# A decode kernel on one core: V pieces ahead of the output projection, turns by group of four, x added late

## The chip, the cores and the metric

One core of a Trainium2 chip. The metric is device time in microseconds (us). A run's time is about 1.7 us longer than the span of its profiled execution, which the views below are cut from; the runs are all of the same (fast) state as far as a single core can tell. Where fractions of a microsecond matter I compare spans and times of day in the profile ("at 1335.4" means 1335.4 us after the span's start).

Words used below. A **piece** is a 4 MB load (K, V or a weight) into one of five slots that are used in turn. A **turn** is the small fp32 matmul step that brings the attention output of a piece from rows to columns (`oT`). **Rows** are the 16 small matmuls (`o_rows`) that then lay it out for the output projection, whose weight is `wo`. V60 to V63 are the last V pieces; wo is 8 MB. `flush()` runs the turns that are pending. PE is TensorE (PEld its weight loads), DVE VectorE, ACT ScalarE, POOL GpSimd; PSUM is the memory that matmuls add up in. The **granted clock** is the share of TensorE's full clock that the trace records.

## The reference

Four decode positions attend to 32 heads and 8192 cached positions each; a gated feed-forward part and x itself are mixed in:

```python
q = (x @ wq)                                     # 4 x 4096, heads of 128
p = softmax(q . k_cache / sqrt(128))             # K and V caches: 4 x 32 x 8192 x 128 bf16, 268 MB each
a = (p . v_cache) @ wo                           # wo: 4096 x 1024
b = x + sigmoid(x . w_r) * ((silu(x @ w_gate) * (x @ w_up)) @ w_down)
out = g * a + (1 - g) * b                        # g = sigmoid(x . gate_w)
```

## The kernel before

The parts that matter. `acc` is one PSUM sum of 4 x 1024 that takes x, the feed-forward part and the output projection.

```python
    def gates():
        # [...] g, 1-g and the sigmoid of x.w_r; then x joins the sum first:
        xf = ttp.tile([Bn, D], F32, name="xf", tag="T")
        nc.vector.tensor_copy(out=xf[:], in_=x6[0:Bn])
        dg = const.tile([Bn, Bn], F32)
        nc.vector.tensor_tensor(out=dg[:], in0=ident[0:Bn, 0:Bn], in1=c12[0:Bn, 0, :], op=ALU.mult)
        for n in range(NH):
            mm_acc(acc[:, n * NB:(n + 1) * NB], dg[:], xf[:, n * NB:(n + 1) * NB], start=True)

    def wo_piece(g0, g1, r0=0, r1=FR):          # one DMA, and a function that uses it
        w = slot()[...]
        nc.sync.dma_start(out=w..., in_=wov[:, g0:g1, r0:r1]...)
        def use():                              # 8 matmuls of 128x512 for each g (1 MB of wo)
            ...
        return use

    def v_piece(u):                             # u = 4 * g + t
        # [...] load; the last V piece in four parts
        o_ps = ops.tile([NM, 4 * Dh], F32, name="o_ps")
        # [...] 32 matmuls into o_ps; flush() after the first 8
        o_sb = osp.tile([NM, 4 * Dh], F32, name="o_sb")
        nc.scalar.copy(out=o_sb[:], in_=o_ps[:])
        def finish():                           # the turn of this piece: 8 rows to 2 columns
            for q in range(4):
                nc.tensor.matmul(oT[:, HT * t:HT * t + HT], lhsT=o_sb[:, q * Dh:(q + 1) * Dh],
                                 rhs=ident[0:NM, q:NM:4], start=(q == 0), stop=(q == 3))
            # [...] after the fourth piece of a group: scale into OT
        pending.append(finish)

    for u in range(NT + LAG):                   # NT = 64, LAG = 4
        if u < NT:
            k_piece(u)
        if u == NT + 1:
            flush()
            o_rows(0, GE)
            wo_piece(0, GS)()                   # 4 MB of wo between V60 and V61
        if u >= LAG:
            v_piece(u - LAG)
        # [...] feed-forward pieces in the first turns
    early = wo_piece(GS, GE)                    # 2 MB
    late = [wo_piece(GE, NWB - 1), wo_piece(NWB - 1, NWB, 0, FR - 1), wo_piece(NWB - 1, NWB, FR - 1, FR)]
    flush()
    early()
    o_rows(GE, NWB)
    for use in late:
        use()
```

Of the kernel before, what the change touches and what calls it, by code (L numbers as in the profile page):

```python
# [9 lines left out]
BF = mybir.dt.bfloat16  # L10
F32 = mybir.dt.float32
U32 = mybir.dt.uint32
ACT = mybir.ActivationFunctionType
ALU = mybir.AluOpType
# [5 lines left out]
def kernel(  # L20
# [22 lines left out]
    nc = tc.nc  # L43
    P = 128
    Bn, Sq, D = A_x.shape
    _, H, Sk, Dh = A_k_cache.shape
    F = B_w_gate.shape[1]
    DT = D // P
    HT = 2
    JR = Sk * HT // P  # L50
    JC = JR // 16
    GT = 4
    GH = GT * HT
# [3 lines left out]
    NT = Bn * H // HT  # L57
    LAG = 4
    FR = 4
    FG = F // (P * FR)  # L60
    NB = 512
# [5 lines left out]
    x2 = A_x.rearrange("b s d -> (b s) d")  # L67
    out2 = out.rearrange("b s d -> (b s) d")

    const = ctx.enter_context(tc.tile_pool(name="const", bufs=1))  # L70
    ring = ctx.enter_context(tc.tile_pool(name="ring", bufs=5))
    ttp = ctx.enter_context(tc.tile_pool(name="ttp", bufs=2))
    ptp = ctx.enter_context(tc.tile_pool(name="ptp", bufs=2))
    osp = ctx.enter_context(tc.tile_pool(name="osp", bufs=2))
    stat = ctx.enter_context(tc.tile_pool(name="stat", bufs=3))
    shrp = ctx.enter_context(tc.tile_pool(name="shrp", bufs=1, space=PSUM))
    accp = ctx.enter_context(tc.tile_pool(name="accp", bufs=1, space=PSUM))
# [1 line left out]
    ops = ctx.enter_context(tc.tile_pool(name="ops", bufs=2, space=PSUM))  # L79
    o2p = ctx.enter_context(tc.tile_pool(name="o2p", bufs=1, space=PSUM))  # L80

    def slot():
        return ring.tile([P, RING], BF, name="piece", tag="piece")
# [3 lines left out]
    x6 = const.tile([NX, D], BF)  # L87
# [7 lines left out]
    ident = const.tile([P, P], F32)  # L95
# [11 lines left out]
    for he in range(4):  # L107
        half, e = divmod(he, 2)
        nc.gpsimd.affine_select(out=R[:, he, :], in_=R[:, he, :], compare_op=ALU.not_equal, fill=1.0,  # L109
                                base=-(64 * half + e), pattern=[[0, 4], [-2, 32]], channel_multiplier=1)  # L110
# [3 lines left out]
                            base=0, pattern=[[-JC, GT], [-32, NQ]], channel_multiplier=1)  # L114
    nc.gpsimd.affine_select(out=m32[:], in_=m32[:], compare_op=ALU.is_ge, fill=0.0,
                            base=JC - 1, pattern=[[JC, GT], [32, NQ]], channel_multiplier=-1)
# [3 lines left out]
    nc.vector.tensor_scalar(out=pen8[:], in0=mask8[:], scalar1=-1.0, scalar2=3.0e38, op0=ALU.add, op1=ALU.mult)  # L120
    nmask8 = const.tile([P, GH], F32)
    nc.vector.tensor_scalar(out=nmask8[:], in0=mask8[:], scalar1=-scale, scalar2=None, op0=ALU.mult)
    ZW = 31 + P + 1
    Zt = [const.tile([P, 4, ZW], BF, name=f"Z{i}") for i in range(2)]
    PB = [const.tile([P, 32, 4, HT, 4], BF, name=f"PB{i}") for i in range(2)]
    for z in Zt + PB:
        nc.gpsimd.memset(z[:], 0.0)  # L127

    qT = const.tile([P, H, Bn], BF)
# [1 line left out]
    OT = const.tile([P, H, Bn], BF)  # L131
    LT = const.tile([P, FR, H // FR, Bn], BF)
    hT = const.tile([P, FG, FR, Bn], BF)
    sgb = const.tile([P, 2, Bn], F32)
# [8 lines left out]
    acc = accp.tile([Bn, D], F32)  # L143

    def mm_acc(out_ap, lhsT, rhs, start=False):
        nc.tensor.matmul(out_ap, lhsT=lhsT, rhs=rhs, start=start, stop=True, skip_group_check=True)  # L146


    def gates():
        wrep = ttp.tile([P, 2, DT, P], BF, name="wrep", tag="T")  # L150
        for i in range(2):
            nc.vector.tensor_copy(out=wrep[:, i, :, :], in_=xw[:, :, Bn + i:Bn + i + 1].to_broadcast([P, DT, P]))
            for t in range(DT):
                mm_acc(rg_ps[:, i, :], wrep[:, i, t, :], xT[t])
        nc.scalar.activation(out=sgb[:], in_=rg_ps, func=ACT.Sigmoid)
        nc.vector.tensor_scalar(out=c12[:, 0, :], in0=sgb[:, 1, :], scalar1=-1.0, scalar2=1.0, op0=ALU.mult, op1=ALU.add)
        nc.vector.tensor_tensor(out=c12[:, 1, :], in0=c12[:, 0, :], in1=sgb[:, 0, :], op=ALU.mult)
        xf = ttp.tile([Bn, D], F32, name="xf", tag="T")
        nc.vector.tensor_copy(out=xf[:], in_=x6[0:Bn])  # L159
        dg = const.tile([Bn, Bn], F32)  # L160
        nc.vector.tensor_tensor(out=dg[:], in0=ident[0:Bn, 0:Bn], in1=c12[0:Bn, 0, :], op=ALU.mult)
        for n in range(NH):
            mm_acc(acc[:, n * NB:(n + 1) * NB], dg[:], xf[:, n * NB:(n + 1) * NB], start=True)


    wqv = A_wq.rearrange("(c t) n -> c t n", t=DT)
# [37 lines left out]
    def wd_piece(g0, ng):  # L204
        w = slot()[:, :ng * FR * D].rearrange("p (g r n) -> p g r n", g=ng, r=FR)
        nc.sync.dma_start(out=w.rearrange("p g r n -> p g (r n)"),
                          in_=wdv[:, g0:g0 + ng].rearrange("f g r n -> f g (r n)"))
        for g in range(ng):
            for r in range(FR):
                for n in range(NH):  # L210
                    mm_acc(acc[:, n * NB:(n + 1) * NB], hT[:, g0 + g, r, :], w[:, g, r, n * NB:(n + 1) * NB])

    WB = P * FR // Dh
    NWB = H // WB

    def o_rows(g0, g1):

        n = g1 - g0
        lp = ops.tile([P, FR, n, Bn], F32, name="o_ps")
        for k in range(WB):  # L220
            for r in range(FR):
                nc.tensor.matmul(lp[32 * k:32 * k + 32, r], lhsT=identb[:, r:P:FR],
                                 rhs=OT[:, WB * g0 + k:WB * g1:WB, :], start=True, stop=True, skip_group_check=True)
        nc.vector.tensor_copy(out=LT[:, :, g0:g1, :], in_=lp[:])

    def wo_piece(g0, g1, r0=0, r1=FR):
        ng, nr = g1 - g0, r1 - r0
        w = slot()[:, :ng * nr * D].rearrange("p (g r n) -> p g r n", g=ng, r=nr)
        nc.sync.dma_start(out=w.rearrange("p g r n -> p g (r n)"),
                          in_=wov[:, g0:g1, r0:r1].rearrange("p g r n -> p g (r n)"))  # L230

        def use():
            for g in range(ng):
                for r in range(nr):
                    for n in range(NH):
                        mm_acc(acc[:, n * NB:(n + 1) * NB], LT[:, r0 + r, g0 + g, :], w[:, g, r, n * NB:(n + 1) * NB])
        return use
# [1 line left out]

    S_ps = {}  # L240
    rinv_t = {}
    oT_t = {}
    pending = []

    def flush():
        while pending:
            pending.pop(0)()

    def heads(u):
        return divmod(u * HT, H)  # L250

    def kv_view(cache, u):
        b, h0 = heads(u)
        return cache[b, h0:h0 + HT].rearrange("h (r j) d -> (h r) (j d)", j=JR)
# [61 lines left out]
    NM = 4 * HT  # L316

    def v_piece(u):
        b, h0 = heads(u)
        g, t = divmod(u, GT)  # L320
        B_ = PB[g % 2]
        vn = slot()
        vv = kv_view(A_v_cache, u)
        cut = 4 if u == NT - 1 else 1
        for c in range(cut):
            lo, hi = c * RING // cut, (c + 1) * RING // cut
            nc.sync.dma_start(out=vn[:, lo:hi], in_=vv[:, lo:hi])
        o_ps = ops.tile([NM, 4 * Dh], F32, name="o_ps")
        n = 0
        for jc in range(JC):  # L330
            for uq in range(4):
                j0 = 16 * jc + 4 * uq
                nc.tensor.matmul(o_ps[:, :], lhsT=B_[:, JC * t + jc, uq].rearrange("p s j -> p (s j)"),  # L333
                                 rhs=vn[:, j0 * Dh:(j0 + 4) * Dh], start=(n == 0), stop=(n == JR // 4 - 1))
                n += 1
                if n == 8:
                    flush()
        o_sb = osp.tile([NM, 4 * Dh], F32, name="o_sb")
        nc.scalar.copy(out=o_sb[:], in_=o_ps[:])  # L339

        def finish():
            if t == 0:
                oT_t[g] = o2p.tile([P, GH], F32, name="oT")
            oT = oT_t[g]
            for q in range(4):
                nc.tensor.matmul(oT[:, HT * t:HT * t + HT], lhsT=o_sb[:, q * Dh:(q + 1) * Dh],  # L346
                                 rhs=ident[0:NM, q:NM:4], start=(q == 0), stop=(q == 3))
            if t == GT - 1:
                oT_t.pop(g)
                hg = h0 + HT - GH  # L350
                nc.vector.scalar_tensor_tensor(out=OT[:, hg:hg + GH, b], in0=oT[:, :], scalar=sgb[:, 1, b:b + 1],  # L351
                                               in1=rinv_t.pop(g)[:], op0=ALU.mult, op1=ALU.mult)
        pending.append(finish)


    gates()
    wq_piece(0)
    wq_piece(TW)
# [1 line left out]
    side = [lambda: gu_piece(wgv, 0, 0), lambda: gu_piece(wgv, 0, TW), lambda: gu_piece(wuv, 1, 0),  # L360
            lambda: (gu_piece(wuv, 1, TW), h_done()), lambda: wd_piece(0, 4), lambda: wd_piece(4, FG - 4)]
    GE = NWB - GH // WB
    GS = GE // 2 + 1
    for u in range(NT + LAG):
        if u < NT:
            k_piece(u)
        if u == NT + 1:
            flush()
            o_rows(0, GE)
            wo_piece(0, GS)()  # L370
        if u >= LAG:
            v_piece(u - LAG)
        if side:
            side.pop(0)()
    early = wo_piece(GS, GE)
    late = [wo_piece(GE, NWB - 1), wo_piece(NWB - 1, NWB, 0, FR - 1), wo_piece(NWB - 1, NWB, FR - 1, FR)]
    flush()
    early()
    o_rows(GE, NWB)
    for use in late:  # L380
        use()
    res = const.tile([Bn, D], BF)
    nc.vector.tensor_copy(out=res[:, 0:NB], in_=acc[:, 0:NB])
# [33 lines left out]
```

## Time and profile before

| | before |
|---|---|
| median of the first 3 runs | 1357.39 us (1356.31 to 1358.82) |
| span of the profiled execution | 1354.7 us |
| PE busy | 1119.6 us, 83% |
| read from HBM | 575.7 MB |

DMA is full in every slice but the last, at about 431 GB/s. The kernel is bound by its load stream, and only the start and the tail can give anything.

The tail in the timeline of PE before (start us, length us, line, operation, count, and in brackets idle time and what ended it):

```profile
1307.48 7.07 PE L146 MATMUL acc<-piece,LT 128*4 128x512 bf16 x32 [0.99 <-DMA piece<-in_A_wo_dram]
1317.20 8.50 PE L333 MATMUL o_ps<-piece,PB_139 128*8 128x512 bf16 x32 [2.65 <-DMA piece<-in_A_v_cache_dram]
1326.42 1.05 PE L346 MATMUL oT<-ident,o_sb 8*128 8x2 f32 x8 [0.72 <-ACT o_sb L339]
1327.40 8.80 PE L333 MATMUL o_ps<-piece,PB_139 128*8 128x512 bf16 x40
...
1337.10 5.34 PE L333 MATMUL o_ps<-piece,PB_139 128*8 128x512 bf16 x24
1343.16 1.05 PE L346 MATMUL oT<-ident,o_sb 8*128 8x2 f32 x8 [0.72 <-ACT o_sb L339]
...
1344.88 6.85 PE L146 MATMUL acc<-piece,LT 128*4 128x512 bf16 x31
```

The first 4 MB of wo are used at 1307.5, V61 at 1317.2, V62 and V63 from 1327.4 to 1342.4, then turn and rows, then the other 32 projection matmuls to 1351.7; result and store take 3 us more.

The last microseconds of the stream, by windows (columns: window, length, busy us and count of PE, PEld, DVE, ACT, POOL, granted clock, DMA share, GB/s):

```profile
1315.00:1320.00 5.00, 2.80 (x7) 0.87 (x7) 0.00 (x0) 0.00 (x0) 0.00 (x0) 0.67 0.98 421
1344.00:1345.00 1.00, 0.67 (x20) 0.56 (x21) 0.29 (x2) 0.00 (x0) 0.00 (x0) 1.00 0.34 133
1345.00:1346.00 1.00, 1.00 (x7) 0.38 (x5) 0.14 (x1) 0.00 (x0) 0.00 (x0) 1.00 0.12 47
1346.00:1347.00 1.00, 1.00 (x6) 0.38 (x5) 0.00 (x0) 0.00 (x0) 0.00 (x0) 1.00 0.09 27
```

The stream ends at about 1346.8, five microseconds before PE does. The first line shows a granted clock of 0.67 on average in a window that begins with idle time (PE had stopped 2.65 us before V61 started at 1317.2); the trace's clock records put half clock from 1316.7 to 1320.1.

### The profile page before, as it was taken

How to read it: one execution, taken by the hardware profiler on the slowest of the kernel's cores; microseconds unless marked ns; L12 is line 12 of the kernel's file. 1: busy time of each engine (PE TensorE's matmuls, PEld its weight loads, DVE VectorE, ACT ScalarE, POOL GpSimd, SP SyncE). 2: the span in 40 equal slices, each digit the busy share in tenths (PEclk: the TensorE clock that was granted, in tenths of full speed). 3: DMA queues.
4: the chain of work that ended last, by engine and by line, in shares of the span. 5: the costliest groups of instructions: out<-in, count | busy, mean ns of one | idle time of the engine just before them, and what ended most of it. 6: DMA issues, size and time to landing. Idle time of an engine off the chain costs nothing.

```text
span 1354.7 us, 12547 instructions
## 1 busy us (share of the span) xinstructions
PE 1119.6 (83%) x5496; PEld 483.1 (36%) x5496; DVE 624.2 (46%) x403; ACT 71.0 (5%) x118; POOL 85.2 (6%) x322
## 2 busy tenths in 40 slices
PE   3765988888787988888888888888888887888888
PEld 2432433333333333333333333333333333333333
DVE  1553445544554454455445534554454445445500
ACT  0001000000000000000000000000000000000000
POOL 1000000000000000000000000000000000000000
PEclk9877989899999998989998999989989999998999
DMA  9999999999999999999999999999999999999996
GB/s 404 428 432 427 427 432 430 433 431 429 430 431 430 433 431 430 429 432 431 430 433 431 430 431 430 429 432 432 431 433 431 432 428 429 431 432 433 432 422 257
DMA packets 21971, 576.50 MB, mean 426 GB/s; under 512 B 2318, under 2 KB 2326, under 8 KB 2588
## 3 DMA queue, kind: packets, MB, share of 16 engines
q1 hardware_dynamic: 21896, 575.68, 99.0%
q8 instruction: 43, 0.70, 0.2%
q14 instruction: 12, 0.10, 0.0%
q10 hardware_dynamic: 20, 0.02, 0.0%
HBM read 575.68 MB, written 0.01 MB: 425 GB/s over the span
## 4 chain that ended last, share of the span: by engine, by line
DMA 48%; PE 33%; DVE 11%; issue 7%; ACT 1%; POOL 0%; DVEq 0%; ACTq 0%; POOLq 0%
DMA piece<-in_A_k_cache_dram 45%; PE o_ps L333 17%; PE S_ps L277 13%; DVE T L270 10%; DMA piece<-in_A_v_cache_dram 3%; PE acc L146 1%; PE oT L346 1%; PE shr L146 1%; ACT o_sb L339 1%; DVE OT L351 0%; DVE xf L159 0%; POOL Z_137 L127 0%; POOL R L109 0%; POOL PB_138 L307 0%; DVEq L270 0%
## 5 line engine op out<-in xcount | busy, mean ns | idle before, releaser
L270 DVE STREAM_TRANSPOSE T<-piece 128x2048 uint32<-128x2048 uint32 x256 | 577.5, 2291 | 506.8 <-DMA piece<-in_A_k_cache_dram 380.7
L277 PE MATMUL S_ps<-T,Z_136 128*128 128x512 bf16 x1024 | 283.6, 431 | 102.2 <-DVE T L270 102.0
L277 PE MATMUL S_ps<-T,Z_137 128*128 128x512 bf16 x1024 | 266.1, 410 | 60.2 <-DVE T L270 60.1
L333 PE MATMUL o_ps<-piece,PB_139 128*8 128x512 bf16 x1024 | 227.7, 381 | 2.7 <-DMA piece<-in_A_v_cache_dram 2.7
L333 PE MATMUL o_ps<-piece,PB_138 128*8 128x512 bf16 x1024 | 226.2, 379 | 0.0
L277 PEld LDWEIGHTS <-Z_136 128*128 128x128 bf16 x1024 | 109.4, 107 | 264.0 <-issue 180.4
L277 PEld LDWEIGHTS <-Z_137 128*128 128x128 bf16 x1024 | 104.3, 103 | 208.8 <-issue 116.9
L333 PEld LDWEIGHTS <-PB_139 128*8 128x8 bf16 x1024 | 86.7, 87 | 139.9 <-issue 16.9
L333 PEld LDWEIGHTS <-PB_138 128*8 128x8 bf16 x1024 | 86.4, 87 | 137.3 <-issue 13.6
L346 PE MATMUL oT<-ident,o_sb 8*128 8x2 f32 x512 | 67.1, 249 | 45.0 <-ACT o_sb L339 45.0
L346 PEld LDWEIGHTS oT<-ident,o_sb 8*128 8x128 f32 x512 | 61.6, 186 | 76.8 <-ACT o_sb L339 76.4
L339 ACT COPY o_sb<-o_ps 8x512 f32<-8x512 f32 x64 | 36.8, 575 | 943.0 <-PE o_ps L333 943.0
L261 POOL COPY Z_137<-qa 32x4 bf16<-32x4 bf16 x128 | 24.9, 194 | 558.1 <-PE S_ps L277 552.5
L261 POOL COPY Z_136<-qa 32x4 bf16<-32x4 bf16 x128 | 24.9, 195 | 554.3 <-PE S_ps L277 533.6
L351 DVE SCALAR_TENSOR_TENSOR OT<-oT,sgb,rinv 128x8 bf16<-128x8 f32 x16 | 3.8, 236 | 90.2 <-PE oT L346 90.2
L146 PEld LDWEIGHTS <-piece 128*128 128x128 bf16 x704 | 22.5, 113 | 4.4 <-issue 3.5
L146 PE MATMUL shr<-xw,piece 128*128 128x4 bf16 x704 | 22.6, 170 | 1.7 <-issue 1.7
L300 ACT ACTIVATE PTs<-S_ps,negm 128x512 bf16<-128x512 f32 x16 | 11.0, 687 | 215.0 <-DVE negm L297 215.0
L302 DVE STREAM_TRANSPOSE PT<-PTs 128x512 bf16<-128x512 bf16 x16 | 11.4, 711 | 13.5 <-ACT PTs L300 13.5
L146 PE MATMUL acc<-piece,LT 128*4 128x512 bf16 x64 | 14.1, 379 | 1.0 <-DMA piece<-in_A_wo_dram 1.0
L313 DVE RECIPROCAL rinv<-tot 128x8 f32<-128x8 f32 x16 | 3.2, 203 | 25.3 <-POOL tot L311 25.3
L146 PE MATMUL acc<-piece,hT 128*4 128x512 bf16 x56 | 12.4, 379 | 0.0
(92 smaller groups left out, 111.0 us busy)
## 6 DMA issues: line engine op xcount, KB each, us to landing
piece<-in_A_k_cache_dram SPq DMA_DIRECT2D x64, 4096.0 KB, 39.2
piece<-in_A_v_cache_dram SPq DMA_DIRECT2D x63, 4096.0 KB, 39.2
piece<-in_A_wq_dram SPq DMA_DIRECT2D x2, 4096.0 KB, 13.1
piece<-in_B_w_gate_dram SPq DMA_DIRECT2D x2, 3584.0 KB, 40.0
piece<-in_B_w_up_dram SPq DMA_DIRECT2D x2, 3584.0 KB
piece<-in_B_w_down_dram SPq DMA_DIRECT2D x1, 4096.0 KB, 39.6
piece<-in_A_wo_dram SPq DMA_DIRECT2D x1, 4096.0 KB
piece<-in_A_v_cache_dram SPq DMA_DIRECT2D x4, 1024.0 KB, 38.5
```

What stands on the lines that cost most here:

```text
L146: nc.tensor.matmul(out_ap, lhsT=lhsT, rhs=rhs, start=start, stop=True, skip_group_check=True)
L261: nc.gpsimd.tensor_copy(out=Z[32 * a:32 * a + 32, :, 31 + 32 * a:32 + 32 * a], in_=qa[32 * a:32 * a + 32, :, h0 + a // QH, b:b + 1])
L270: nc.vector.transpose(out=T[:].rearrange("p j h i e -> p (j h i e)").bitcast(U32), in_=kn[:, c * CJ * Dh:(c + 1) * CJ * Dh].bitcast(U32))
L277: nc.tensor.matmul(sps[:, :], lhsT=Z[:, he, s:s + P], rhs=T[:, 16 * jl:16 * jl + 16, half, :, e], start=(t == 0 and jc == 0 and he == 0), ...
L300: nc.scalar.activation(out=PTs[:], in_=sps[:], func=ACT.Exp, bias=negm[:, 0:1], scale=scale, accum_out=rs[:, 0:1])
L302: nc.vector.transpose(out=PT[:].rearrange("p j i -> p (j i)"), in_=PTs[:])
L313: nc.vector.reciprocal(out=rinv[:], in_=tot[:])
L333: nc.tensor.matmul(o_ps[:, :], lhsT=B_[:, JC * t + jc, uq].rearrange("p s j -> p (s j)"), rhs=vn[:, j0 * Dh:(j0 + 4) * Dh], start=(n == 0) ...
L339: nc.scalar.copy(out=o_sb[:], in_=o_ps[:])
L346: nc.tensor.matmul(oT[:, HT * t:HT * t + HT], lhsT=o_sb[:, q * Dh:(q + 1) * Dh], rhs=ident[0:NM, q:NM:4], start=(q == 0), stop=(q == 3))
L351: nc.vector.scalar_tensor_tensor(out=OT[:, hg:hg + GH, b], in0=oT[:, :], scalar=sgb[:, 1, b:b + 1], in1=rinv_t.pop(g)[:], op0=ALU.mult, op ...
```

## The change

Its intent: let the V pieces end early, so that turn and rows are done while wo streams, and then follow the wo stream to its end; make one turn per group of four pieces in place of four; take x out of the start. In V, piece t of a group now writes PSUM partitions 32t to 32t+7, the copies of a group fill one SBUF tile, and a selection matrix `selg` turns all four at once.

```diff
+    selg = const.tile([P, 4, GT, HT], F32)            # ones that pick rows 32t + 4s + q
+    OS = [const.tile([P, 4 * Dh], F32, name=f"OS{i}") for i in range(2)]
@@ gates @@
-        xf = ttp.tile([Bn, D], F32, name="xf", tag="T")
-        nc.vector.tensor_copy(out=xf[:], in_=x6[0:Bn])
-        for n in range(NH):
-            mm_acc(acc[...], dg[:], xf[...], start=True)
+    def add_x():                                      # loads x again, casts it, 2 matmuls
+        [...]
@@ feed-forward @@
+        # [...] its first matmuls now start the sum (start=True), as x no longer does
@@ v_piece @@
-                nc.tensor.matmul(o_ps[:, :], lhsT=B_[...],
+                nc.tensor.matmul(o_ps[32 * t:32 * t + NM, :], lhsT=B_[...],
-        o_sb = osp.tile([NM, 4 * Dh], F32, name="o_sb")
-        nc.scalar.copy(out=o_sb[:], in_=o_ps[:])
+        o_sb = OS[g % 2]
+        nc.scalar.copy(out=o_sb[32 * t:32 * t + NM, :], in_=o_ps[32 * t:32 * t + NM, :])
+        if t < GT - 1:
+            return
             for q in range(4):
-                nc.tensor.matmul(oT[:, HT * t:HT * t + HT], lhsT=o_sb[...], rhs=ident[0:NM, q:NM:4], ...)
+                nc.tensor.matmul(oT[:, :], lhsT=o_sb[...], rhs=selg[:, q]..., ...)
@@ the tail @@
-        if u == NT + 1:
-            flush()
-            o_rows(0, GE)
-            wo_piece(0, GS)()
+        if u == NT:                                   # after V60
+            o_rows(0, GE)
+            add_x()
-    early = wo_piece(GS, GE)
-    late = [wo_piece(GE, NWB - 1), ...]
+    last = [wo_piece(0, GS), wo_piece(GS, GE), wo_piece(GE, NWB - 1),      # 4, 2, 1 MB,
+            wo_piece(NWB - 1, NWB, 0, FR - 1), wo_piece(NWB - 1, NWB, FR - 1, FR)]   # 768, 256 KB
     flush()
-    early()
     o_rows(GE, NWB)
-    for use in late:
+    for use in last:
         use()
```

## The prediction

> **What bounds the kernel now.** The DMA stream. The page's DMA row is at nine tenths in every slice but the last, at about 431 GB/s; 575.7 MB at that rate is 1336 of 1354.7 us. The Trainium skill, "DMA: Bandwidth & Descriptors", Specifications, gives a fabric ceiling of 435 GB/s; this trace sits 1% under it. Issue to landing is 39.2 us, four pieces of 9.7 us: the queue is never empty. Only start and tail can give time.
>
> The tail, by the timeline: the stream ends near 1346 (133 GB/s in 1344 to 1345, then 15). V62 and V63 run on PE from 1327.4 to 1342.4; then copy (0.57), turn (eight fp32 passes, 1.05), OT (0.23), rows (0.5), and the last 32 matmuls of the output projection, 0.219 us each, 1344.7 to 1351.75. Result and store: 3 us.
>
> **What changes.**
> 1. 64 turns of 1.05 us, each with 0.7 us of waiting for the ACT copy, become 16. That frees some 80 us of PE, all inside the DMA stream: worth 0.
> 2. x leaves the start: 2.2 us of DVE and 3.6 us of PE (20.0 to 23.5), with pieces queued ahead; worth 0. It returns after V60, where PE has 2.7 us of slack per V piece (7.0 of 9.7); its 8 KB load lands with V60. Cost 0.
> 3. The tail's order. Bytes are the same, so the stream still ends near 1346.5. The last quarter of V63 lands near 1327, PE ends V63 near 1331, the turn and rows near 1334. But all 64 projection matmuls now stand behind the V pieces, where before 32 ran ahead of V61 (1307.5 to 1314.5). The first 4 MB of wo land two pieces after V61's old place: 1317.2 + 19.4 = 1336.6. From there PE needs 64 x 0.219 = 14.0 us, DMA 9.7 for the rest: PE binds, ending at 1350.7 at full clock.
> 4. The clock. PE has almost nothing to do from 1331 to 1336.6. Before V61, 2.65 idle us were followed by eight matmuls at 0.43 us, granted clock 0.67. The Trainium skill, "TensorE: Matmul & The Clock Gate", What's actually happening, has windows of 3.4 us; this trace's clock falls in such steps. I expect one half-speed stretch at the start of the wo matmuls: estimate 0.5 to 1.7 us. PE then ends at 1351.2 to 1352.4, against 1351.75.
>
> So the gain from moving V earlier is spent: the turn leaves the end, but the whole projection queues behind a 4 MB landing. Net -1 to +0.6 us.
>
> **Predicted time:** 1357.3 us, range 1354.8 to 1359.6. Chances: faster by over 2% 0.01, within 2% 0.98, slower 0.01.
>
> **What would show each step.** DMA rate unchanged, its end within 1 us. PE busy falls by 45 to 55 us, the oT group from 512 to 128 records. V63's last matmul near 1331. PE waits for the first wo piece until about 1336.6, then 64 matmuls back to back to about 1352, the first ones slow; the last wo piece lands well before its use.
>
> **What would make it wrong.** The clock staying full at the end (1 to 2 us better); the slower DMA engines ending at another time, since their spread over the last 7 us sets every late landing; x's load landing late and holding V61 on PE; outputs at partitions 32, 64, 96 making V's matmuls slower or faster than 7.0 us a piece; run-to-run spread, 2.5 us among three runs before.

## More of the kernel before

The page's rows of busy time, DMA busy share (tenths) and GB/s in 40 slices, the queue that fetches instructions (packets, MB, share), and the group of the turns (columns: line, engine, operation, tiles, shape and count, then busy us and mean ns, then idle time before and its releaser):

```profile
PE 1119.6 (83%) x5496; PEld 483.1 (36%) x5496; DVE 624.2 (46%) x403; ACT 71.0 (5%) x118; POOL 85.2 (6%) x322
DMA  9999999999999999999999999999999999999996
GB/s 404 428 432 427 427 432 430 433 431 429 430 431 430 433 431 430 429 432 431 430 433 431 430 431 430 429 432 432 431 433 431 432 428 429 431 432 433 432 422 257
q8 instruction: 43, 0.70, 0.2%
L346 PE MATMUL oT<-ident,o_sb 8*128 8x2 f32 x512 | 67.1, 249 | 45.0 <-ACT o_sb L339 45.0
```

## The result, and the profile after

| | before | after |
|---|---|---|
| median of 4 runs | 1358.04 us (1356.31 to 1358.82) | 1356.53 us (1356.32 to 1356.58) |
| ratio | 1 | 0.999 (95% interval 0.9973 to 1.0008) |
| span of the profiled execution | 1354.7 us | 1354.6 us |
| PE busy | 1119.6 us | 1065.1 us |

Ratios are the mean time of one kernel's fast runs over that of the other's of the same rounds, so not quite the ratio of the medians beside them. The time lies inside the stated range. What follows rests on landings and times in the traces, and on intervals of ratios that are narrower than 2%.

The same rows of the page after:

```profile
PE 1065.1 (79%) x5112; PEld 434.5 (32%) x5112; DVE 622.3 (46%) x403; ACT 71.0 (5%) x118; POOL 86.8 (6%) x326
DMA  9999999999999999999999999999999999999996
GB/s 403 429 431 430 425 430 432 432 432 431 429 432 430 433 430 431 427 431 432 431 433 432 433 428 432 430 428 433 431 433 430 432 428 430 432 431 433 432 419 258
q8 instruction: 40, 0.66, 0.2%
L355 PE MATMUL oT<-selg,OS_139 128*128 128x8 f32 x64 | 8.5, 259 | 5.7 <-ACT OS_139 L348 5.7
L355 PE MATMUL oT<-selg,OS_138 128*128 128x8 f32 x64 | 8.5, 259 | 5.7 <-ACT OS_138 L348 5.7
```

PE lost 54.5 us of work (1119.6 less 1065.1), most of it turns (67.1 became 17.0), and the stream ran at the same rate: the busy time taken from an engine that waits for the stream is worth nothing where it was. (That its instructions cost something is shown further down.)

PE's timeline in the tail after:

```profile
1309.02 19.80 PE L342 MATMUL o_ps<-piece,PB_143 128*8 128x512 bf16 x96
1329.54 1.06 PE L355 MATMUL oT<-selg,OS_139 128*128 128x8 f32 x8 [0.72 <-ACT OS_139 L348]
1330.93 0.33 PE L232 MATMUL o_ps<-OT,identb 128*32 128x8 bf16 x16 [0.33 <-DVE OT L358]
1335.42 16.26 PE L150 MATMUL acc<-piece,LT 128*4 128x512 bf16 x64 [4.16 <-DMA piece<-in_A_wo_dram]
```

V61 to V63 end at 1328.8 in place of 1342.4, as meant. Then PE waits 4.16 us for the first 4 MB of wo and runs all 64 projection matmuls in a row, to 1351.68; before it ended at 1351.73. The windows of that stretch, and of the stream's end:

```profile
1335.00:1338.00 3.00, 2.58 (x7) 0.78 (x7) 0.00 (x0) 0.00 (x0) 0.00 (x0) 0.50 0.93 384
1338.00:1340.00 2.00, 2.00 (x6) 0.57 (x5) 0.00 (x0) 0.00 (x0) 0.00 (x0) 0.50 0.69 285
1344.00:1345.00 1.00, 1.00 (x6) 0.39 (x5) 0.00 (x0) 0.00 (x0) 0.00 (x0) 1.00 0.29 111
1345.00:1346.00 1.00, 1.00 (x6) 0.42 (x5) 0.00 (x0) 0.00 (x0) 0.00 (x0) 1.00 0.00 0
```

Two things to see. The clock is at half for the first 4.7 us of the projection: the clock records of this trace have one stretch of half clock here, from 1333.25 to 1340.07, which is 6.83 us. And the stream is over by about 1345.3 (no traffic in the window from 1345), where before it ran to about 1346.8: the same bytes ended 1.4 us earlier. I had not predicted that.

### The profile page after: what moved, and what is told of

Its sections match the earlier page's. It is cut to its first block, busy times and chain, and to the rows that moved or that the text cites. A ratio compares the mean times of both kernels' runs of the same rounds, so it can differ in the third digit from the quotient of the medians.

```text
span 1354.6 us, 11809 instructions
## 1 busy us (share of the span) xinstructions
PE 1065.1 (79%) x5112; PEld 434.5 (32%) x5112; DVE 622.3 (46%) x403; ACT 71.0 (5%) x118; POOL 86.8 (6%) x326
## 4 chain that ended last, share of the span: by engine, by line
DMA 47%; PE 31%; DVE 12%; issue 7%; POOL 2%; ACT 1%; DVEq 0%; SPq 0%; ACTq 0%
DMA piece<-in_A_k_cache_dram 45%; PE o_ps L342 16%; PE S_ps L286 12%; DVE T L279 10%; DMA piece<-in_A_wo_dram 3%; PE acc L150 2%; PE oT L355 1%; DVE PT L311 1%; PE shr L150 1%; POOL PB_142 L316 1%; POOL PB_143 L316 1%; POOL tot L320 0%; ACT OS_138 L348 0%; ACT OS_139 L348 0%; DVE OT L358 0%
## 5 line engine op out<-in xcount | busy, mean ns | idle before, releaser
L348 ACT COPY OS_138<-o_ps 8x512 f32<-8x512 f32 x32 | 18.5, 577 | 594.2 <-PE o_ps L342 594.2
L348 ACT COPY OS_139<-o_ps 8x512 f32<-8x512 f32 x32 | 18.5, 577 | 536.8 <-PE o_ps L342 536.8
L355 PE MATMUL oT<-selg,OS_139 128*128 128x8 f32 x64 | 8.5, 259 | 5.7 <-ACT OS_139 L348 5.7
L355 PE MATMUL oT<-selg,OS_138 128*128 128x8 f32 x64 | 8.5, 259 | 5.7 <-ACT OS_138 L348 5.7
L316 POOL COPY PB_143<-PT 64x512 bf16<-64x512 bf16 x8 | 8.3, 1032 | 65.9 <-DVE rex L318 65.9
```

What stands on the lines that cost most here:

```text
L316: nc.gpsimd.tensor_copy(out=B_[W:P, :, :, 1, :], in_=Pv[W:P])
L348: nc.scalar.copy(out=o_sb[32 * t:32 * t + NM, :], in_=o_ps[32 * t:32 * t + NM, :])
L355: nc.tensor.matmul(oT[:, :], lhsT=o_sb[:, q * Dh:(q + 1) * Dh], rhs=selg[:, q].rearrange("p t s -> p (t s)"), start=(q == 0), stop=(q == 3))
```

## The experiments

My theory (A) before the runs: the kernel ends where PE ends, and PE ends 64 matmuls after the landing of one 4 MB piece. Rivals: the end of the stream sets the end whatever its order is (B); only the half clock costs (C); the new order wins some microseconds and another part of the change loses them (D). The first eight kernels ran in two batches, each batch on one chip with its own runs of the kernel before. The record marks every run as correct, the two that are wrong too, so that mark tells little about this part of the result; the split kernels are right because their edit only divides loads.

### Split the first wo load

In the changed kernel, four DMAs of 1 MB into the same tile, used as they land:

```diff
-        nc.sync.dma_start(out=w..., in_=wov[:, g0:g1, r0:r1]...)
+        for c in range(0, ng, step or ng):
+            e = min(c + (step or ng), ng)
+            nc.sync.dma_start(out=w[:, c:e]..., in_=wov[:, g0 + c:g0 + e, r0:r1]...)
-    last = [wo_piece(0, GS), ...
+    last = [wo_piece(0, GS, step=1), ...
```

> The changed kernel with its first 4 MB of wo loaded in four parts of 1 MB into the same tile. Theory A (the end is PE: 64 projection matmuls, two stretches of half clock among them, queue behind one 4 MB landing at 1335.4): the parts land 7.3, 4.9 and 2.4 us earlier, PE starts near 1328 to 1331 and stays at full clock, the second piece (2 MB) is used when it lands near 1340.3 and PE ends near 1347.5 instead of 1351.7: span 1350.4, 4 us less than the changed kernel, ratio to before about 0.996. Rival B (the end of the DMA stream sets the end, whatever stands in it): no change, span 1354.6. Rival C (only the clock costs): -2.2 us.

Measured: median 1351.94 us against 1356.35 us, ratio 0.9965 (0.9953 to 0.9978), span 1350.2. PE's timeline:

```profile
1331.05 6.85 PE L150 MATMUL acc<-piece,LT 128*4 128x512 bf16 x31
1340.24 7.07 PE L150 MATMUL acc<-piece,LT 128*4 128x512 bf16 x32 [2.34 <-DMA piece<-in_A_wo_dram]
```

The first 32 matmuls now start right after the rows, the other 32 begin when the next 2 MB land, and PE ends at 1347.3 in place of 1351.7. B falls: bytes and order are the same and 4.4 us are gone. C falls too, as its 2.2 us are too few. The clock stayed full here (63 matmuls in 6.85 and 7.07 us), so about 2.3 of the 4.4 us are the clock's, as the busy-wait experiment below measures it, and about 2.1 come from not queueing behind one landing.

### Split all of wo

```diff
-    last = [wo_piece(0, GS, step=1), wo_piece(GS, GE), ...
+    last = [wo_piece(0, GS, step=1), wo_piece(GS, GE, step=1), ...
```

> As the kernel with the first piece split, and the next 2 MB of wo in two parts too. Theory A: PE now follows the DMA landings 1 MB at a time, the last 256 KB land near 1345.4 and are two matmuls: PE ends 1346 to 1346.7, span 1349.0 to 1349.7, 5 us less than the changed kernel, ratio to before 0.995. This is also the candidate that beats both. Rival B: no change. Rival C: -2.2 us.

Measured: median 1351.27 us, ratio 0.9961 (0.9948 to 0.9973), span 1349.4. PE's timeline:

```profile
1330.96 8.68 PE L150 MATMUL acc<-piece,LT 128*4 128x512 bf16 x39
1340.22 1.89 PE L150 MATMUL acc<-piece,LT 128*4 128x512 bf16 x8 [0.58 <-DMA piece<-in_A_wo_dram]
1342.70 3.78 PE L150 MATMUL acc<-piece,LT 128*4 128x512 bf16 x16 [0.59 <-DMA piece<-in_A_wo_dram]
```

PE now waits about 0.6 us for each of two parts and ends at 1346.5, 1.3 us after the last landing (1345.2). From here on a late landing sets the time: PE's last wait ends when the seventh MB of wo has landed (1342.65), and the last 16 matmuls follow without a wait. This is the fastest correct version.

### Keep PE busy while it waits

In the changed kernel, wo loaded as it was:

```diff
     o_rows(GE, NWB)
+    spare = ops.tile([P, 512], F32, name="o_ps")
+    for _ in range(17):
+        nc.tensor.matmul(spare[:], lhsT=identb[:], rhs=PB[0][...], start=True, stop=True)   # never read
```

> The changed kernel with 17 matmuls of no use (128x512, result never read) after the second row step, so that PE is busy from about 1331.3 to 1335.0 while it waits for the first 4 MB of wo. Theory A: the clock stays full, 64 matmuls take 14.0 instead of 16.3 us from the landing at 1335.4, PE ends near 1349.5: -2.2 us, span 1352.4. Rival B: no change, span 1354.6. Rival C: -2.2 us as A; with the two split kernels it tells C from A.

Measured: median 1353.88 us, ratio 0.9981 (0.9968 to 0.9995), span 1352.3.

```profile
1331.60 3.84 PE L387 MATMUL o_ps<-PB,identb 128*128 128x512 bf16 x17
1335.37 13.97 PE L150 MATMUL acc<-piece,LT 128*4 128x512 bf16 x64
```

The first wo piece lands at the same time (1335.4), and the 64 matmuls take 13.97 in place of 16.26 us. So the half clock costs the changed kernel 2.3 us of its end, and useless work removes that cost.

### Leave the last 4 MB of wo out

The result is wrong: the last 32 matmuls read the first piece.

```diff
-        w = slot()[...]; nc.sync.dma_start(...)
+        if g0 == 0:                       # only the first piece is loaded
+            w = slot()[...]; nc.sync.dma_start(...); first["w"] = w
+        w = first["w"]
```

> The changed kernel without the loads of the last 4 MB of wo; their 32 matmuls read the first piece instead (result wrong on purpose). Theory A: the first piece lands at the same time or up to 1 us earlier, PE runs the same 64 matmuls behind it: span within 1 us of 1354.6 although 4 MB, 9.7 us of the stream, are gone. Rival B: the stream ends 9.7 us earlier and so does the kernel: span about 1345.

Measured: median 1355.44 us, ratio 0.9993 (0.998 to 1.0005), span 1354.6, as the changed kernel's.

```profile
1335.36 16.31 PE L150 MATMUL acc<-piece,LT 128*4 128x512 bf16 x64 [4.12 <-DMA piece<-in_A_wo_dram]
```

Taking 4 MB, 9.7 us of the stream, out of the end is worth nothing in this execution. It was the slowest of the five (1356.38 us; the others took 1355.33 to 1355.92), so up to about 1 us of the 9.7 may have been won, and no more. That is the plainest proof that in the changed kernel the end of the stream does not set the end. B is dead.

### One part of the change at a time

The changed kernel again, for comparison on the same chip:

> The changed kernel again, on the chip of the three kernels that make one part of the change each, for comparison: span 1354.6 to 1354.9, ratio to before 0.998 to 1.0.

Measured: median 1356.48 us against 1357.51 us, ratio 0.9992 (0.9979 to 1.0004), span 1355.0.

The order of the tail alone (turns by piece and x first as before; the `u == NT` block without `add_x()` and the `last` list of the change):

> The kernel before with the new order of the tail alone: V60 to V63 first, all of wo behind them; turns after each V piece and x at the start as before. Theory A: the end is the landing of the first 4 MB of wo plus 16.3 us of matmuls, so it ends as the changed kernel does, within 0.7 us (span 1354 to 1355.5). Rival D (the order wins some us and the turn by group or the late x loses them again): span 1349 to 1352.

Measured: median 1357.13 us, ratio 0.9999 (0.9987 to 1.0012), span 1356.7.

```profile
1336.79 16.86 PE L146 MATMUL acc<-piece,LT 128*4 128x512 bf16 x64 [2.40 <-DMA piece<-in_A_wo_dram]
```

This profiled execution missed my expectation by 1.2 us. It was the slowest of five; the spans of the other four are 1355.0 to 1356.0 us, three of them inside. The shape is A's (64 matmuls behind one landing), but the landing is at 1336.79 where the full change has 1335.42, 1.4 us later, and the clock cost 0.6 us more. The 1336.6 of my prediction would have been right for this kernel.

The turn by group alone (the diff of `v_piece`, `selg` and `OS`, nothing else):

> The kernel before with the turn by group alone; order of the tail and x as before. Theory A: some 54 us of PE go, all inside the DMA stream and worth nothing there; at the end the turns of V61 and V62 leave the chain from V62's landing (1326.9) to the end: -0.5 to -1.8 us, span 1353 to 1354.2. Rival D: slower by some us.

Measured: median 1355.84 us, ratio 0.9985 (0.9971 to 0.9998), span 1354.1.

```profile
1340.85 1.06 PE L349 MATMUL oT<-selg,OS 128*128 128x8 f32 x8 [0.72 <-ACT OS L342]
...
1342.72 8.38 PE L150 MATMUL acc<-piece,LT 128*4 128x512 bf16 x31
```

The last turn comes 2.3 us earlier than before (1343.16), but the last 31 matmuls take 8.38 in place of 6.85 us: the clock records have half clock from 1342.4 to 1345.8. Why it fell there no run shows: PE's idle times just before (0.72 and 0.33 us) are the same in the kernel before, which kept full clock there.

x late alone:

> The kernel before with x joining late alone (after the first row step, ahead of the first use of wo). Theory A: the PE time that leaves the start was hidden and what returns falls into a wait for DMA: within 0.7 us of before, 1354.0 to 1355.4 span. Rival D: slower by some us, with V61 or the first use of wo starting later than in before by as much.

Measured: median 1357.37 us, ratio 0.9994 (0.9982 to 1.0007), span 1354.0. No loss is seen (the interval leaves room for about 1 us, not for the several of D), so D falls for all three parts. The profiled execution is one of the quicker of its five runs (1355.71 to 1357.56), so I read no gain from its span.

### Why the stream's end moved: the instruction count

The 1.4 us went with the turn by group: the last landing is at 1346.8, 1346.7 and 1346.6 in the three kernels with a turn by piece (before, order only, x only) and at 1345.2 to 1345.4 in all those above with a turn by group and all loads. Here is when each of the 16 DMA engines' shares of the last 256 KB landed, in us after the first of them, sorted, from the trace's record of landings. I put the kernels of the next experiments beside it:

```
                 PE packets   first at   the 16 shares, us after the first
before               43       1337.3     0.0 0.0 0.4 1.3 1.4 1.4 3.2 5.9 | 7.6 7.7 7.7 7.7 7.8 7.9 9.4 9.5
after                40       1337.3     0.0 0.1 0.4 1.3 1.4 2.8 3.0 6.6 | 7.6 7.6 7.7 7.7 7.7 8.0 8.0 8.1
tiny matmuls, 7      43       1337.1     0.0 0.1 0.3 1.4 1.4 2.3 2.7 5.9 | 7.7 7.8 7.8 7.9 8.0 9.4 9.5 9.7
tiny matmuls, 23     50       1337.3     0.0 0.0 0.2 1.2 1.2 2.2 2.9 6.0 | 9.2 9.2 9.3 9.3 9.5 9.5 10.9 10.9
half of V's work     32       1337.1     0.0 0.1 0.3 1.3 1.5 2.3 2.9 5.8 | 6.2 6.2 6.3 6.3 6.3 6.4 6.5 6.5
```

The fastest engine ends at the same time everywhere; the eight slowest are behind it in steps of about 1.5 us. Across the run the lags of these eight grow by such steps, one engine after another. (The other eight spread too, the slowest of them to about 6 us; that does not follow the packets, and I did not look for its cause.) The trace shows the packets of the instruction queue to be 16 KB each, 1.06 us long on average, about one per 256 PE instructions of the program. So theory F: each such packet holds one of eight engines up by about 1.5 us, the packets go round these eight, and since a load is used only when all 16 shares have landed (the last share of the first 4 MB of wo at 1335.38, PE's start at 1335.42), the engine with the most packets sets every late landing. 40 packets are five for each of eight; the 43 of before (42 of them ahead of the end) are six for two of them. Which engine a packet ran on is not in the records that I have; the count of eight is read from the lags.

The same records test the count inside a run. In the kernel before, when 41 packets had started (a load whose first share landed at 1288.0), one share was at 9.5 us and the seven before it at 7.7 to 8.0; with 42 (at 1324.8) two were at 9.4 and 9.5. In two kernels above, the 40th packet came too late for the last landing (without the last 4 MB: it started at 1338.6, the last landing was at 1335.3; turn by group alone: it started at 1343.2), and there seven shares are at 7.5 to 8.0 us and the eighth is at 6.2 and 6.4. So 39 packets already charge the step that 40 do.

The Trainium skill, "Runtime: NRT & Kernel Launch", Instruction fetch mechanics, says that instructions are fetched by DMA "in 16 KiB blocks (256 instructions)" and that the cost of a block boundary is "mostly hidden". The size agrees with this trace; the cost is not hidden here, where the loads themselves are the bound, as the next runs show.

I tested it on the kernel with all of wo split, where a late landing sets the time. First that kernel again, on the chip of the three that follow:

> The kernel with all of wo split, again, on the chip of the three kernels that change its number of PE instructions. 40 instruction packets, last landing of the stream near 1345.2, span 1349.4, ratio to before 0.996.

Measured: median 1351.24 us against 1357.59 us, ratio 0.9958 (0.9945 to 0.997), span 1349.7.

Then 784 useless PE instructions more, none in the last eight V pieces:

```diff
+        for _ in range(7 if u < NT - 8 else 0):            # in v_piece, ahead of the copy
+            c0 = 32 * ((t + 1) % GT)                       # rows of o_ps that nobody reads
+            nc.tensor.matmul(o_ps[c0:c0 + 32, 0:4], lhsT=identb[:, 0:32], rhs=identb[:, 0:4],
+                             start=True, stop=True, skip_group_check=True)
```

> The kernel with all of wo split plus 7 tiny matmuls of no use in each of the first 56 V pieces (392 matmuls and as many weight loads, into rows of the PSUM tile that nobody reads; PE has time for them). Theory F (each instruction packet, of which PE's program needs one per 256 instructions, holds one of eight DMA engines up for 1.5 us; the engine with most packets sets the last landing): 43 packets, so some engines get six instead of five: the last landing and the span are 1.5 us later, 1346.7 and 1350.9, although nothing near the end is touched. Rival G (the stream ended 1.4 us earlier with the turn by group because of what PE or ACT did with their time near the end): no change, span 1349.4.

Measured: median 1352.68 us, ratio 0.9968 (0.9956 to 0.9981), span 1351.0; three of the eight slow engines are a step further behind and the last landing is at 1346.8, 1.4 us later than in the kernel without them (1345.4).

```profile
1332.54 15.52 PE L150 MATMUL acc<-piece,LT 128*4 128x512 bf16 x63
```

In this profile PE does not wait for any of these landings: it runs 63 matmuls in a row, with half clock from 1333.5 to 1336.9, and reaches the seventh MB of wo shortly after that landed (1344.26). So here it is the landing that bears F out; that the span agrees too is in part chance.

The same with 23 in place of 7:

> As the last with 23 tiny matmuls in each of the first 56 V pieces (2576 instructions more). Theory F: 50 packets, so one or two of the eight engines get seven: last landing near 1348.2, span 1352.4, 3 us later than without them. Rival G: no change, span 1349.4. Rival H (a cost in proportion to the number of packets on every engine, not a count on the worst engine): 10 packets of 1.05 us over 16 engines, +0.7 us.

Measured: median 1354.20 us, ratio 0.998 (0.9967 to 0.9992), span 1352.4; two engines are at the step of seven packets, last landing 1348.2.

And 2048 instructions fewer, by leaving out every second V matmul (`range(0, 4, 2)` for the inner loop; the result is wrong, all loads stay):

> The kernel with all of wo split and every second matmul of each V piece left out (result wrong on purpose, loads unchanged): 2048 PE instructions fewer. Theory F: 32 packets, four per engine: last landing near 1343.7, span 1347.9, 1.5 us earlier. Rival G: no change in the landing, span 1349.4. Rival H: -0.5 us.

Measured: median 1349.61 us, ratio 0.9946 (0.9933 to 0.996), span 1347.9; all eight at the step of four packets, last landing 1343.6.

Instruction packets on the pages of these four (split again, 7, 23, half of V), each followed by its span line:

```profile
q8 instruction: 40, 0.66, 0.2%
span 1349.7 us, 11813 instructions
```

```profile
q8 instruction: 43, 0.70, 0.2%
span 1351.0 us, 12597 instructions
```

```profile
q8 instruction: 50, 0.82, 0.2%
span 1352.4 us, 14389 instructions
```

```profile
q8 instruction: 32, 0.52, 0.2%
span 1347.9 us, 9765 instructions
```

The stream's end in the windows of the kernel with 23 tiny matmuls, and then of the one with half of V's work:

```profile
1346.00:1347.00 1.00, 1.00 (x7) 0.35 (x5) 0.00 (x0) 0.00 (x0) 0.00 (x0) 1.00 0.16 66
1347.00:1348.00 1.00, 1.00 (x5) 0.32 (x4) 0.00 (x0) 0.00 (x0) 0.00 (x0) 1.00 0.09 33
```

```profile
1343.00:1344.00 1.00, 0.99 (x6) 0.42 (x5) 0.00 (x0) 0.00 (x0) 0.00 (x0) 1.00 0.02 6
1344.00:1345.00 1.00, 0.90 (x5) 0.17 (x2) 0.27 (x1) 0.06 (x1) 0.00 (x0) 1.00 0.00 0
```

Four kernels, packet counts of 32, 40, 43 and 50, spans of 1347.9, 1349.7, 1351.0 and 1352.4, all within 0.3 us of what F said; the last landings are 1343.6, 1345.4, 1346.8 and 1348.2. Rival G (something that the turns did near the end) falls, since nothing near the end was touched in the two kernels with tiny matmuls. Rival H (a cost spread evenly over 16 engines) gives 0.7 us for ten packets, and 2.7 to 3.0 were measured. F stands as a count on the worst engine: for three packets it charges a whole step, and 39 and 40 cost the same. One rival was not separated by an experiment: these kernels also give PE more or less work, not only more or fewer instructions. Against it stand the lags: the fastest eight shares hardly move between the five kernels of the table (the slowest of them is at 5.8 to 6.6 us), and the other eight move by whole steps, as many as the packet count says.

## Why the prediction was right or wrong

The time and the main mechanism were right. Two terms of the sum were mis-sized and cancelled; that the end of PE came out nearly unchanged, as predicted, is partly luck.

- *The DMA stream bounds; PE work freed inside it is worth nothing.* Right for the rate: 54.5 us of PE went and the GB/s row did not move.
- *"That frees some 80 us of PE, all inside the DMA stream: worth 0."* Wrong: it moved the late landings by 1.4 us. 48 turns fewer are 768 PE instructions fewer, three instruction packets fewer, and the slowest DMA engine ended a step earlier. The first wo piece landed at 1335.4, not 1336.6. I had named the spread of the slow engines as a risk but had not asked what makes it.
- *x late costs 0.* No loss seen, 0.9994 (0.9982 to 1.0007). The 8 KB load landed in time: x's matmuls ran from 1307.2 for 1.88 us in the changed kernel, ahead of V61.
- *V63 ends near 1331, all 64 matmuls behind the 4 MB landing, 14.0 us from there at full clock.* Right: V63 ended at 1328.8, PE ended 64 matmuls after the landing, and with the clock held up these took 13.97 us. Leaving out the 4 MB behind it won about 1 us at most, and splitting it gave 4.4 us.
- *"I expect one half-speed stretch ... 0.5 to 1.7 us."* The mechanism was right, the size was not: I had counted one step of 3.4 us, and the stretch was two (6.83 us), of which 4.7 us fell on the projection and cost 2.3 us (16.26 less 13.97). Half-clock stretches in the traces before and after last whole multiples of 3.41 us (most of them 3.41 or 6.83), but for the one that the end cuts off. Why it was two steps stays open. V ended two microseconds earlier than I thought, but that is not shown to be the reason: in the kernel with the new order alone V63 ended at 1332.0, PE waited 2.40 us, and the stretch was 6.83 us as well. The Trainium skill, "TensorE: Matmul & The Clock Gate", Why this matters for your kernels, advises no PE-idle gap above about 3 us; the 4.16 us gap here agrees, and before had a half-speed stretch around a gap of only 2.65 us.
- *Net -1 to +0.6 us at the end of PE.* Measured -0.05 us (1351.73 to 1351.68): the landing 1.2 us earlier than I said, the clock 0.6 us or more dearer.

About 5 us were to be had from the change: they were turned into a wait for a 4 MB landing and a half clock, and cutting the loads of wo into parts of at most 1 MB gives them back (1351.2 us, 0.996 of before). How much of that the new order would give without the turn by group was not run; the kernel with 7 tiny matmuls, which has the 43 packets of before, took 1352.7 us.

What stays open: runs of the kernel before spread over 2.5 us (1356.31 to 1358.82; 0.7 and 3.4 us on the chips of the second and third group of experiments) and those of the changed kernel in the first comparison over 0.3 us. A clock that falls in other places from run to run would do that; no run here tests it.

## What to carry to other kernels

When work is moved to stand behind the last loads, it moves only to the landing of the load it reads: cut the last loads so that each part's compute is shorter than the next part's transfer, and the tail follows the stream by one small part. Look at whether the engine that waits there comes back at full clock. And in a kernel bound by loads, count instructions: the packets that fetch them share the DMA engines, and the unluckiest engine sets when the last load has landed.

## What the Trainium skill lacked or had wrong

- "Runtime: NRT & Kernel Launch", Instruction fetch mechanics, calls the cost of a 16 KiB boundary mostly hidden. In a load-bound kernel each packet of PE's program put one DMA engine about 1.5 us behind, in steps on eight of the 16; with 32, 40, 43 and 50 packets the last load landed at 1343.6, 1345.4, 1346.8 and 1348.2 us. No page gives a size for what instruction fetch takes from loads.
- "DMA: Bandwidth & Descriptors" gives no size for the spread between engines: nothing there says that the 16 shares of one load can land 8.0 to 10.9 us apart at the end of a long stream, as in every kernel here that keeps all its work.
- "TensorE: Matmul & The Clock Gate", Why this matters for your kernels, puts the danger at idle gaps of about 3 us or more. Here half clock came with a gap of 2.65 us (before V61 in the kernel before) and with one of 2.40 us (order alone), and did not come with one of 2.34 us (first load split, before the second half of wo). So a gap under 3 us was not safe; what decides it was not tested.
